# Where the weight clamps of two fused mixers run: VectorE for the first mixer, POOL a step ahead for the second

## The chip, the cores and the metric

One core of a Trainium2 chip runs the whole program. Times are device microseconds (us) of one launch. The kernel before takes 677.71 us (median of 3 runs, 677.46 to 679.39). The core's engines are TensorE (PE, with its weight loads as PEld), VectorE (DVE), ScalarE (ACT), GpSimd (POOL) and SyncE (SP, which here issues every DMA). Each engine takes its own instructions strictly in order; engines wait for one another through semaphores.

## The reference

Shapes: batch 4, 8 heads, 768 tokens, 48 numbers a head; DM = 384, FF1 = 1024, FF2 = 1536.

```
# 1 attention: a decaying state per head
for t in range(S):
    cur = u * k_t (outer) v_t;  y_t = r_t . (state + cur);  state = w * state + k_t (outer) v_t
# 2 first mixer
h = max(x @ w_in, 0);  conv = sum of 3 taps of h along the tokens, weights conv_w
x = (h * sigmoid(conv)) @ w_out
# 3 second mixer
xn = (x - mean) / sqrt(var + 1e-6) * g_ln
out = x + max(xn @ w_ch1, 0) @ w_ch2
```

The inputs of the mixers' weights are 64-bit floating point numbers, which no engine multiplies. They are loaded as pairs of 32-bit words, and the kernel makes 32-bit numbers of them itself.

## The kernel before

The 3072 tokens are 24 tiles of 128 for attention (`attn_tile`, `state_update`) and 8 blocks of 384 for the mixers. All of attention and of the first mixer comes first, interleaved: block j of `mixer1` starts when its three tiles are done, and `step()` pushes the attention of later tiles in between. The results of the first mixer go to DRAM (`x1_dram`). Then the second mixer (`mixer2`) runs over the 8 blocks. It loads each block back (`x1b`, three pieces, `prefetch`), normalises it (`norm`: statistics on DVE, the power -1/2 on POOL as `rs`, the scaled `xn` on DVE), transposes it on PE (`pxt`) and multiplies.

A product of two 32-bit matrices is made of three PE products: each operand is split in a high part that PE takes exactly (`wih`, `woh`, `c1h`, `c2h`, and `xh`, `gh`, `rh`) and a low rest (`wil` and so on).

Weights come in 22 pieces (`wjob`), in this order: three pieces of the first half of w_in (512 columns), one of w_out (`wo_0`), three of the second half of w_in, three of w_out, six of w_ch1 (`c1`), six of w_ch2 (`c2`). All but the w_in pieces are 768 wide. A piece is loaded by SP into a staging tile `st` and then decoded in `wdec` by: ACT, absolute value of the high word read as a 32-bit number; POOL, a clamp to a range (`magnitude`, line 115); DVE, two shifts in one instruction (TENSOR_SCALAR), then two instructions that merge in the low word and the sign (SCALAR_TENSOR_TENSOR); ACT, the rounded high part; DVE, the low rest. The three conv taps go the same way once (`conv_weights`, 24 wide).

Order of this work: `wdo(count, last)` runs so many steps of the current piece, `need(job)` runs steps until a piece is done. In the code before, a piece is three steps, and its ACT and POOL instructions are written right behind the last decode step of the piece ahead of it (`ahead`). After four tiles of attention `wdo` has done the three first w_in pieces and `wo_0`. In block 0 `need` holds features 4 to 7 (`psm` number 4 and on) until the second half of w_in is ready. Instructions that go through `vo`, `ao`, `so`, `go` and all of PE keep the order in which they are written; between them a scheduler places the rest of each engine's instructions beforehand. `ps_m`, `ps_c` and `ps_a` are the PSUM pools.

Of the kernel before, what the change touches and what calls it, by code (L numbers as in the profile page):

```python
# [10 lines left out]
I32 = mybir.dt.int32  # L11
AF = mybir.ActivationFunctionType
ALU = mybir.AluOpType
# [3 lines left out]
DM = H * D  # L17
# [3 lines left out]
NF1 = FF1 // 128  # L21
NF2 = FF2 // 128
# [9 lines left out]
WN = 768  # L32
# [5 lines left out]
W_MIN = 2.0 ** -15 * 1.125  # L38
W_MAX = float.fromhex("0x1.dffcp+16")
# [4 lines left out]
def body(ctx, tc, r, k, v, w, u, w_in, conv_w, w_out, g_ln, w_ch1, w_ch2, out):  # L44
# [4 lines left out]
    io = ctx.enter_context(tc.tile_pool(name="io", bufs=2))  # L49
# [23 lines left out]
    vo = InOrder(nc.vector)  # L73
# [34 lines left out]
    def words(st, n):  # L108
        return [st[:, 0:2 * n].rearrange("p (n two) -> p n two", two=2)[:, :, i] for i in range(2)]

    def magnitude(st, n):

        t = ap.tile([128, WN], F32, tag="wd", name="wdec", bufs=2)[:, 0:n]
        ao.activation(out=t, in_=words(st, n)[1].bitcast(F32), func=AF.Abs)
        go.tensor_scalar(out=t, in0=t, scalar1=W_MIN, scalar2=W_MAX, op0=ALU.max, op1=ALU.min)
        return t

    def decode(st, n, t):
# [9 lines left out]

    wjobs = []

    def wjob(src, n, hi, lo, scale=None):

        st, mag = [], []

        def load():
            st.append(io.tile([128, 2 * WN], I32, tag="st", name="st", bufs=3))
            dst = st[0][:, 0:2 * n]
            if len(src.shape) == 3:
                dst = dst.rearrange("p (a n) -> p a n", a=src.shape[1])
            so.dma_start(out=dst, in_=src.bitcast(I32))  # L140

        def ahead():
            if not mag:
                mag.append(magnitude(st[0], n))

        def steps():
            ahead()
            t = mag[0]
            yield from decode(st[0], n, t)
            if me + 1 < min(len(wjobs), w_loaded[0]):  # L150
                wjobs[me + 1][2]()
            if len(src.shape) == 3:
                t = t.rearrange("p (a n) -> p a n", a=src.shape[1])
            kw = {} if scale is None else {"scale": gl[:, scale:scale + 1]}
            ao.activation(out=hi, in_=t, func=AF.Copy, **kw)
            yield
            if scale is None:
                vo.tensor_tensor(out=lo, in0=t, in1=hi.bitcast(F32), op=ALU.subtract)
            else:
                vo.scalar_tensor_tensor(out=lo, in0=t, scalar=kw["scale"], in1=hi.bitcast(F32),  # L160
                                        op0=ALU.mult, op1=ALU.subtract)
        me = len(wjobs)
        wjobs.append((load, steps(), ahead))
        return len(wjobs) - 1

    wi_job, wo_job, c1_job, c2_job = {}, {}, {}, {}

    def rows2(w_, f):
        return w_[f * 128:f * 128 + 256, :].rearrange("(a p) d -> p a d", p=128)

    def wi_half(f0):
        for kt in range(KT):
            wi_job[f0 // 512] = wjob(w_in[kt * 128:kt * 128 + 128, f0:f0 + 512], 512,
                                     wih[:, kt, f0:f0 + 512], wil[:, kt, f0:f0 + 512])

    def wo_rows(f):
        wo_job[f] = wo_job[f + 1] = wjob(rows2(w_out, f), 2 * DM, woh[:, f:f + 2, :], wol[:, f:f + 2, :])

    wi_half(0)
    wo_rows(0)  # L180
# [13 lines left out]
    def wload(count):  # L194

        while w_loaded[0] < min(count, len(wjobs)):
            wjobs[w_loaded[0]][0]()
            w_loaded[0] += 1

    def wdo(count=1, last=None):  # L200

        for _ in range(count):
            while w_done[0] < (len(wjobs) if last is None else last + 1):
                wload(w_done[0] + 2)
                if next(wjobs[w_done[0]][1], "end") != "end":
                    break
                w_done[0] += 1
# [436 lines left out]
        return cst  # L644

    def conv_weights(cst):
        t = magnitude(cst, 3 * NF1)
        yield from decode(cst, 3 * NF1, t)
        v_.tensor_copy(out=cw, in_=t.rearrange("p (k f) -> p k f", k=3))

# [36 lines left out]
    decayed_k(0)  # L687
    while finished[0] < EARLY - 1:
        step()
        wdo(2, wo_job[0])  # L690
    for _ in conv_weights(cst):
        pass
    ahead, pace = [iter(())], [0]
    for j in range(NB):
        slot = [0]
        while finished[0] < min((j + 1) * TT - (j % 2), NT - 1):
            step()

        def before1(f):
            if f < NF1:  # L700
                need(wi_job[f // 4])
            if f >= LAG - 1:
                need(wo_job[f - LAG + 1])

        def after1(f):
            slot[0] += 1
            pace[0] += 2 if j else 1.9
            if j == 1:
                pace[0] += 0.4
            if pace[0] >= 5:  # L710
                pace[0] -= 5
                step()
            if j == 0:
                wdo(2, wo_job[NF1 - 1])
            elif j < NB - 2:
                wdo(slot[0] % 4 == 0, c1_job[NF2 - 1])
            else:
                wdo(slot[0] % 3 == 0, c2_job[4])
            if j == NB - 1:
                if slot[0] == 1:  # L720
                    ahead[0] = prefetch(0)
                elif slot[0] >= 7:
                    next(ahead[0], None)

        mixer1(xT[j], spill(j), before1, after1)
# [55 lines left out]
```

## Time and profile before

| what | value |
|---|---|
| median of the runs | 677.71 us |
| the profiled execution: its time, its span | 680.46 us, 678.7 us |
| busy: PE, DVE, ACT, POOL | 634.3, 434.7, 268.9, 123.1 us |
| chain that ended last, by engine | PE 62%, DVE 26%, ACT 4%, issue 3%, DMA 2%, POOL 1% |
| POOL clamps of 768, of 512 columns | 16 of 3024 ns and 6 of 2350 ns in the mean |

The span is what the profiler shows between the first and the last instruction; the 1.76 us between it and the execution's time lie around it. A row of the trace's timeline gives the start in us, the duration, the engine, the line of the code, the instruction, what it writes and reads, how many in a row, and in brackets how long the engine stood idle before it and what ended that.

### The profile page before, as it was taken

The page shows a single profiled execution, that of the slowest core. Times are in us where ns is not written, and L with a number is a line of the kernel's source. Part 1 is how long each engine was busy: PE and PEld are TensorE (multiplying, and loading weights), DVE is VectorE, ACT ScalarE, POOL GpSimd, SP SyncE. Part 2 cuts the span into 40 slices and gives each one's busy share as a digit, 9 for nine tenths or more (in the row PEclk, how much of TensorE's full clock was granted, in tenths as well). Part 3 has the DMA queues.
Part 4 walks back from the last instruction along what each step waited for, and adds up shares of the span by engine and source line. Part 5 has one row for each costly group of instructions (what it writes and reads, how often), then busy time and mean ns, then how long its engine had stood idle before and what let it go on. Part 6 is the DMA issues. An engine that isn't in the chain of part 4 may idle for free.

```text
span 678.7 us, 12382 instructions
## 1 busy us (share of the span) xinstructions
PE 634.3 (93%) x5100; PEld 606.8 (89%) x5100; DVE 434.7 (64%) x823; ACT 268.9 (40%) x537; POOL 123.1 (18%) x136
## 2 busy tenths in 40 slices
PE   3758599999989999999999999999999999999996
PEld 3647488899978989999899999999999999999996
DVE  5998999998999899986999624142332415242211
ACT  1436556646565556666675312112121212112110
POOL 5452540412131312301215000000000000000000
PEclk9779699999999999999999999999999999999998
DMA  8964433333334322303033001020201002020001
GB/s 173 181 156 114 150 94 82 67 96 84 84 91 97 82 75 69 94 1 117 1 129 117 0 13 59 1 70 1 71 1 46 25 1 71 1 70 1 36 1 39
DMA packets 93841, 45.14 MB, mean 67 GB/s; under 512 B 80337, under 2 KB 89682, under 8 KB 93778
## 3 DMA queue, kind: packets, MB, share of 16 engines
q1 hardware_dynamic: 93778, 44.28, 25.1%
q8 instruction: 42, 0.69, 0.4%
q14 instruction: 21, 0.17, 0.1%
HBM read 34.83 MB, written 9.44 MB: 65 GB/s over the span
## 4 chain that ended last, share of the span: by engine, by line
PE 62%; DVE 26%; ACT 4%; issue 3%; DMA 2%; POOL 1%; SPq 0%; DVEq 0%; POOLq 0%
PE psm L70 28%; PE acc L70 28%; DVE c L410 6%; DVE wdec L70 4%; DVE aT L285 3%; DVE gl L397 3%; DVE c L391 2%; PE yps L70 2%; DMA x1b<-x_dram 2%; PE dps L70 1%; DVE rT L262 1%; PE pxt L70 1%; POOL wdec L70 1%; DVE av L270 1%; DVE kks L238 1%
## 5 line engine op out<-in xcount | busy, mean ns | idle before, releaser
L424 DVE SCALAR_TENSOR_TENSOR rl<-psm,rh 128x384 fp32r<-128x384 f32 x96 | 53.3, 555 | 142.6 <-ACT rh L423 142.6
L423 ACT ACTIVATE rh<-psm 128x384 fp32r<-128x384 f32 x96 | 47.2, 492 | 207.9 <-PE psm L70 207.9
L70 PE MATMUL psm<-xnh,c1h 128*128 128x384 f32 x288 | 99.0, 344 | 0.1
L70 PE MATMUL psm<-xnh,c1l 128*128 128x384 f32 x288 | 97.5, 338 | 0.0
L70 PE MATMUL acc<-c2h,rh 128*128 128x384 f32 x288 | 97.1, 337 | 0.0
L70 PE MATMUL acc<-c2l,rh 128*128 128x384 f32 x288 | 97.1, 337 | 0.0
L70 PE MATMUL acc<-c2h,rl 128*128 128x384 f32 x288 | 97.0, 337 | 0.0
L70 PE MATMUL psm<-xnl,c1h 128*128 128x384 f32 x288 | 96.9, 337 | 0.0
L410 DVE SCALAR_TENSOR_TENSOR c<-h,cw,c 128x384 f32<-128x384 f32 x128 | 84.5, 661 | 9.1 <-ACT c L408 8.1
L70 POOL TENSOR_SCALAR wdec<-wdec 128x768 f32<-128x768 f32 (+2 forms) x23 | 62.8, 2729 | 115.2 <-ACT wdec L70 93.6
L70 PE MATMUL psm<-xh,wih 128*128 128x386 f32 x192 | 68.9, 359 | 10.7 <-ACT wih L70 7.8
L70 PE MATMUL acc<-woh,gh 128*128 128x384 f32 x192 | 67.4, 351 | 2.3 <-DVE xl L309 1.5
L70 PE MATMUL acc<-woh,gl 128*128 128x384 f32 x192 | 65.6, 341 | 2.7 <-DVE gl L397 2.7
L70 PE MATMUL psm<-xl,wih 128*128 128x386 f32 x192 | 66.2, 345 | 0.0
L70 PE MATMUL psm<-xh,wil 128*128 128x386 f32 x192 | 66.2, 345 | 0.0
L70 PE MATMUL acc<-wol,gh 128*128 128x384 f32 x192 | 65.2, 340 | 0.0
L447 POOL TENSOR_TENSOR rs<-rs,nhalf 128x1 f32<-128x1 f32 x24 | 15.4, 658 | 227.8 <-DVE rs L446 226.4
L390 ACT ACTIVATE c<-c 128x384 f32<-128x384 f32 x64 | 33.5, 524 | 56.2 <-DVE c L410 56.0
L70 PEld LDWEIGHTS psm<-xnh,c1h 128*128 128x128 f32 x288 | 54.3, 189 | 0.4 <-DVE ok L658 0.4
L70 PEld LDWEIGHTS psm<-xnl,c1h 128*128 128x128 f32 x288 | 54.4, 189 | 0.0
L70 PEld LDWEIGHTS psm<-xnh,c1l 128*128 128x128 f32 x288 | 54.2, 188 | 0.0
L70 PEld LDWEIGHTS acc<-c2l,rh 128*128 128x128 f32 x288 | 54.1, 188 | 0.0
(104 smaller groups left out, 1162.1 us busy)
## 6 DMA issues: line engine op xcount, KB each, us to landing
st<-in_moe_w_ch_dram SPq DMA_DIRECT2D x12, 768.0 KB, 4.9
rvbuf<-in_r_dram SPq DMA_DIRECT2D x24, 192.0 KB, 2.9
kt<-in_k_dram SPq DMA_DIRECT2D x24, 192.0 KB, 3.5
rvbuf<-in_v_dram SPq DMA_DIRECT2D x24, 192.0 KB, 3.1
x_dram<-x SPq DMA_DIRECT2D x24, 192.0 KB, 1.9
x1b<-x_dram SPq DMA_DIRECT2D x24, 192.0 KB, 2.9
out_dram<-x1b SPq DMA_DIRECT2D x24, 192.0 KB, 1.9
st<-in_moe_w_in_dram SPq DMA_DIRECT2D x6, 512.0 KB, 5.9
```

Source lines behind the costliest of these rows:

```text
L70: return lambda *args, **kw: tc.keep_in_program_order(op(*args, **kw))
L238: v_.tensor_tensor(out=kks[:, n % 2, :, :, 0:D], in0=loaded[n][1].unsqueeze(1).to_broadcast([128, 2, H, D]), in1=tku, op=ALU.mult)
L262: v_.tensor_tensor(out=rT, in0=prt[0:PR], in1=tr, op=ALU.mult)
L270: v_.tensor_tensor(out=av, in0=kks[:, n % 2, 1, :, 0:D], in1=rt[:, :, 0:D], op=ALU.mult)
L285: v_.copy_predicated(out=aT[:, q], mask=later.bitcast(I32), data=dps[q])
L390: a_.activation(out=st["c"], in_=st["c"], func=AF.Sigmoid)
L391: v_.tensor_tensor(out=st["c"], in0=st["h"][:, 1:T + 1], in1=st["c"], op=ALU.mult)
L397: v_.tensor_tensor(out=st["gl"], in0=st["c"], in1=st["gh"].bitcast(F32), op=ALU.subtract)
L410: v_.scalar_tensor_tensor(out=c, in0=h[:, o:o + T], scalar=cw[:, tap, f:f + 1], in1=c, op0=ALU.mult, op1=ALU.add)
L423: a_.activation(out=gh, in_=ps[:, 0:T], func=AF.Relu)
L424: v_.scalar_tensor_tensor(out=gl_, in0=ps[:, 0:T], scalar=0.0, in1=gh.bitcast(F32), op0=ALU.max, op1=ALU.subtract)
L447: g_.tensor_tensor(out=rs[:, 1:2], in0=rs[:, 0:1], in1=nhalf, op=ALU.pow)
```

## The change

The clamp's engine becomes an argument. The ten pieces of the first mixer and the conv taps give it to DVE; the twelve pieces of the second mixer keep POOL. `ahead` is gone: every piece has a fourth step, which starts it with the absolute value and the clamp, and the piece's decode steps follow in later calls. Pieces of the second mixer are staged in a single tile of their own (`sc`) in place of the three of `st`, and the next one's load is issued in the step of the third decode instruction. The paces of `wdo` change with the step count, and before the first block `wdo` now stops after the three first w_in pieces.

```diff
-    def magnitude(st, n):
+    def magnitude(st, n, clamp):
...
-        go.tensor_scalar(out=t, in0=t, scalar1=W_MIN, scalar2=W_MAX, op0=ALU.max, op1=ALU.min)
+        clamp.tensor_scalar(out=t, in0=t, scalar1=W_MIN, scalar2=W_MAX, op0=ALU.max, op1=ALU.min)
...
-    def wjob(src, n, hi, lo, scale=None):
+    def wjob(src, n, hi, lo, scale=None, clamp=None):
...
-            st.append(io.tile([128, 2 * WN], I32, tag="st", name="st", bufs=3))
+            st.append(io.tile([128, 2 * WN], I32, tag="st" if clamp else "sc", name="st", bufs=3 if clamp else 1))
...
-        def ahead():
-            if not mag:
-                mag.append(magnitude(st[0], n))
-
         def steps():
-            ahead()
-            t = mag[0]
+            t = magnitude(st[0], n, clamp or go)
+            yield
             yield from decode(st[0], n, t)
-            if me + 1 < min(len(wjobs), w_loaded[0]):
-                wjobs[me + 1][2]()
+            if clamp is None:
+                wload(me + 2)
...
     (wi_half and wo_rows: wjob(..., clamp=vo))
...
-                wload(w_done[0] + 2)
+                wload(w_done[0] + (2 if w_done[0] < wo_job[NF1 - 1] else 1))
...
-        t = magnitude(cst, 3 * NF1)
+        t = magnitude(cst, 3 * NF1, vo)
...
-        wdo(2, wo_job[0])
+        wdo(2, wi_job[0])
...
-                wdo(slot[0] % 4 == 0, c1_job[NF2 - 1])
+                wdo(slot[0] % 3 == 0, c1_job[NF2 - 1])
             else:
-                wdo(slot[0] % 3 == 0, c2_job[4])
+                wdo(slot[0] % 2 == 0, c2_job[4])
```

PE's matmuls stand in the same order before and after. What moves on the other engines is shown at three places. The rows give the line, the instruction, what it writes and reads, and its shape; numbers only tell instances of a name apart.

First place: DVE up to the third piece of w_in's second half, which `psm` number 4 needs. Before, the last two of the three pieces are `wdec_645` and `wdec_711`; `c` and `gl` belong to the gates of features 1 to 3.

```order
L70 SCALAR_TENSOR_TENSOR wdec_645<-st_640,wdec_645 128x512
L397 TENSOR_TENSOR gl_824<-c_733,gh_823 128x384
L391 TENSOR_TENSOR c_818<-h_817,c_818 128x384
L70 TENSOR_TENSOR wil_97<-wdec_645,wih_96 128x512
L70 TENSOR_SCALAR wdec_711<-wdec_711 128x512
L397 TENSOR_TENSOR gl_892<-c_818,gh_891 128x384
L70 SCALAR_TENSOR_TENSOR wdec_711<-st_650,wdec_711 128x512 x2
L70 TENSOR_TENSOR wil_97<-wdec_711,wih_96 128x512
```

After, the three pieces are `wdec_695`, `wdec_727` and `wdec_807`, and each begins with two TENSOR_SCALAR, the clamp and the shifts.

```order
L70 SCALAR_TENSOR_TENSOR wdec_695<-st_627,wdec_695 128x512
L387 TENSOR_TENSOR c_795<-h_794,c_795 128x384
L70 SCALAR_TENSOR_TENSOR wdec_695<-st_627,wdec_695 128x512
L258 TENSOR_TENSOR rT_828<-prt_823,tr_85 112x512
L393 TENSOR_TENSOR gl_881<-c_795,gh_880 128x384
L70 TENSOR_TENSOR wil_97<-wdec_695,wih_96 128x512
L70 TENSOR_SCALAR wdec_727<-wdec_727 128x512 x2
L70 SCALAR_TENSOR_TENSOR wdec_727<-st_693,wdec_727 128x512 x2
L70 TENSOR_TENSOR wil_97<-wdec_727,wih_96 128x512
L70 TENSOR_SCALAR wdec_807<-wdec_807 128x512 x2
L70 SCALAR_TENSOR_TENSOR wdec_807<-st_725,wdec_807 128x512 x2
L70 TENSOR_TENSOR wil_97<-wdec_807,wih_96 128x512
```

The clamps have joined DVE's queue, and the last two pieces stand back to back with no gate work between them. The decoding of `wo_0`, which stood ahead of the first `psm`, now stands ahead of these three pieces. Up to the last row DVE's queue holds the same instructions before and after, but for the eight clamps (six of 512, one of 768, one of 24 columns).

Second place: POOL from the end of the first mixer into the second. `rs` is the power of a block's normalisation, `wdec` the clamp of a c2 piece; before:

```order
L70 TENSOR_SCALAR wdec_4135<-wdec_4135 128x768
L70 TENSOR_SCALAR wdec_4335<-wdec_4335 128x768
L70 TENSOR_SCALAR wdec_4468<-wdec_4468 128x768
L447 TENSOR_TENSOR rs_4579<-rs_4579,nhalf_90 128x1
L447 TENSOR_TENSOR rs_4617<-rs_4617,nhalf_90 128x1
L447 TENSOR_TENSOR rs_4655<-rs_4655,nhalf_90 128x1
L70 TENSOR_SCALAR wdec_4518<-wdec_4518 128x768
```

After:

```order
L70 TENSOR_SCALAR wdec_4437<-wdec_4437 128x768
L70 TENSOR_SCALAR wdec_4510<-wdec_4510 128x768
L443 TENSOR_TENSOR rs_4575<-rs_4575,nhalf_90 128x1
L443 TENSOR_TENSOR rs_4616<-rs_4616,nhalf_90 128x1
L443 TENSOR_TENSOR rs_4655<-rs_4655,nhalf_90 128x1
L744 TENSOR_LOAD general_91
L70 TENSOR_SCALAR wdec_4569<-wdec_4569 128x768
```

The two clamps that stand ahead of block 1's three powers are those of the fourth and fifth c2 piece in both. Before, they were staged in tiles of three (`wdec_4335`, `wdec_4468`); after, one by one in the single tile (`wdec_4437`, `wdec_4510`). A read of the flag that chooses a fallback path (TENSOR_LOAD) has come in behind the powers. SP's queue at the same place, where `st` is a c2 piece's load, `x_dram` the store of the last block of the first mixer, and `x1b` the load of block 1; before:

```order
L655 DMA wr<-in_w_dram 1x384
L70 DMA st<-in_moe_w_ch_dram 128x2x768 x2
L681 DMA x1b<-x_dram 128x384 x3
L675 DMA x_dram<-x_4507 128x384
L675 DMA x_dram<-x_4509 128x384
L675 DMA x_dram<-x_4511 128x384
L748 TENSOR_LOAD general
```

After:

```order
L651 DMA wr<-in_w_dram 1x384
L70 DMA st<-in_moe_w_ch_dram 128x2x768
L744 TENSOR_LOAD general
L744 ISA x2
L671 DMA x_dram<-x_4500 128x384
L671 DMA x_dram<-x_4502 128x384
L671 DMA x_dram<-x_4504 128x384
L70 DMA st<-in_moe_w_ch_dram 128x2x768
L677 DMA x1b<-x_dram 128x384 x3
```

The load of the fifth c2 piece (the second `st` after) and the loads of block 1 have moved behind the flag and the three stores. The other engines read the flag in mid-stream now too, PE among its matmuls of block 0.

Third place: DVE at the normalisation of block 0, which runs in the last block of the first mixer. `xn` is the scaled piece that PE's first `pxt` transposes, `c` a tap of a gate. Before (first two of the three `xn`):

```order
L449 TENSOR_SCALAR xn_4221<-x1b_4095,mv_4215,rs_4216 128x384
L410 SCALAR_TENSOR_TENSOR c_4023<-h_4022,cw_88,c_4023 128x384
L449 TENSOR_SCALAR xn_4248<-x1b_4096,mv_4242,rs_4243 128x384
L397 TENSOR_TENSOR gl_3994<-c_3952,gh_3993 128x384
L70 TENSOR_TENSOR c2l0_118<-wdec_3560,c2h0_112 128x768
```

After:

```order
L70 TENSOR_SCALAR wdec_4115<-wdec_4115 128x768
L406 SCALAR_TENSOR_TENSOR c_4163<-h_4162,cw_88,c_4163 128x384
L442 TENSOR_SCALAR rs_4283<-mv_4282 128x1
L406 SCALAR_TENSOR_TENSOR c_4204<-h_4203,cw_88,c_4204 128x384
L445 TENSOR_SCALAR xn_4220<-x1b_4097,mv_4214,rs_4215 128x384
L393 TENSOR_TENSOR gl_4169<-c_4131,gh_4168 128x384
```

The first `xn` has moved behind the first tap of `c_4204`, the gate of the matmul group that PE does last ahead of the first `pxt`; before, that tap (`c_4205`) stands some 30 rows behind it.

## Rows read from the trace of the kernel before

**Rows 1.** Stages: stretch, length, busy PE, PEld, DVE, ACT, POOL, PEclk, DMA, GB/s.

```profile
20.00:49.50 29.50, 18.81 (x305) 15.19 (x302) 26.66 (x45) 10.98 (x22) 17.90 (x17) 0.78 0.81 157
49.50:76.70 27.20, 17.68 (x155) 15.35 (x155) 23.70 (x47) 15.66 (x29) 8.15 (x6) 0.81 0.45 123
...
100.00:320.00 220.00, 214.19 (x2312) 198.56 (x2312) 200.90 (x343) 131.63 (x272) 45.97 (x42) 1.00 0.32 80
...
365.00:678.00 313.00, 307.41 (x1776) 306.01 (x1774) 106.83 (x239) 61.11 (x122) 17.56 (x23) 0.99 0.09 29
```

**Rows 2.** Waits of PE: what waited for what, us in total, times, longest.

```profile
PE psm L70 <- ACT wih L70: 7.8, 2, 5.2
PE psm L70 <- POOL xl L315: 2.8, 1, 2.8
```

**Rows 3.** The same, of 320 to 678 us alone.

```profile
PE acc L70 <- DVE gl L397: 1.0, 1, 1.0
```

**Rows 4.** Timeline: first block's start, last high part of w_in, DVE behind it.

```profile
49.47 0.69 PE L70 MATMUL psm<-xh,wih 128*128 128x386 f32 x1 [2.85 <-POOL xl L315]
...
76.03 0.63 ACT L70 ACTIVATE wih<-wdec 128x512 fp32r<-128x512 f32 x1 [1.72 <-DVE wdec L70]
...
76.69 0.69 DVE L70 TENSOR_TENSOR wil<-wdec,wih 128x512 fp32r<-128x512 f32 x1 [0.69 <-ACT wih L70]
```

**Rows 5.** Timeline of DVE: shifts of 512 columns and the row behind.

```profile
28.50 0.41 DVE L70 TENSOR_SCALAR wdec<-wdec 128x512 int32<-128x512 int32 x1
28.83 0.54 DVE L270 TENSOR_TENSOR av<-kks,rvbuf 128x384 f32<-128x384 f32 x1
```

**Rows 6.** Timeline: DVE rows beside a POOL instruction, and rows of their form alone.

```profile
21.77 1.38 DVE L70 TENSOR_SCALAR wdec<-wdec 128x512 int32<-128x512 int32 x1 [0.83 <-POOL wdec L70]
23.18 0.97 DVE L70 SCALAR_TENSOR_TENSOR wdec<-st,wdec 128x512 int32<-128x512 int32 x1
25.30 0.67 DVE L70 SCALAR_TENSOR_TENSOR wdec<-st,wdec 128x512 int32<-128x512 int32 x1
53.95 1.64 DVE L410 SCALAR_TENSOR_TENSOR c<-h,cw,c 128x384 f32<-128x384 f32 x2 [2.63 <-ACT c L408]
61.38 1.14 DVE L410 SCALAR_TENSOR_TENSOR c<-h,cw,c 128x384 f32<-128x384 f32 x2
74.39 3.00 POOL L70 TENSOR_SCALAR wdec<-wdec 128x768 f32<-128x768 f32 x1 [5.05 <-ACT wdec L70]
74.80 1.19 DVE L70 SCALAR_TENSOR_TENSOR wdec<-st,wdec 128x512 int32<-128x512 int32 x1
```

**Rows 7.** Timeline at block 0's normalisation: the gate's first product, the first transpose.

```profile
343.38 0.64 ACT L408 ACTIVATE c<-h,cw 128x384 f32<-128x384 f32 x1
343.57 0.49 PE L70 MATMUL pxt<-ident,xn 128*128 128x128 f32 x3
```

**Rows 8.** Timeline at block 1's normalisation; then the c2 load's landing.

```profile
366.45 1.38 SPq L675 DMA_DIRECT2D x_dram<-x  x3
368.60 0.46 DVE L449 TENSOR_SCALAR xn<-x1b,mv,rs 128x384 f32<-128x384 f32 x1
370.14 0.72 POOL L447 TENSOR_TENSOR rs<-rs,nhalf 128x1 f32<-128x1 f32 x1 [1.03 <-DVE general L661]
371.13 0.91 ACT L70 ACTIVATE wdec<-st 128x768 f32<-128x768 f32 x1
372.11 0.49 ACT L423 ACTIVATE rh<-psm 128x384 fp32r<-128x384 f32 x1
372.13 2.82 POOL L70 TENSOR_SCALAR wdec<-wdec 128x768 f32<-128x768 f32 x1 [1.28 <-ACT wdec L70]
376.65 0.49 PE L70 MATMUL pxt<-ident,xn 128*128 128x128 f32 x3
```

**Rows 9.** DMA issues of 350 to 385 us: KB each, median us to landing.

```profile
st<-in_moe_w_ch_dram SPq DMA_DIRECT2D x1, 768.0 KB, 4.5
```

**Rows 10.** PE's read of the flag: shortest, median, longest ns; first, last start.

```profile
L748 PEldq TENSOR_LOAD <-general x1: 487/487/487, 669.3 to 669.3; - x1
```

More of the change, by code (lines that the diff above doesn't have):

```diff
@@ L129, in body @@
     wjobs = []
-    def wjob(src, n, hi, lo, scale=None):
-        st, mag = [], []
+    def wjob(src, n, hi, lo, scale=None, clamp=None):
+        st = []
         def load():
-            st.append(io.tile([128, 2 * WN], I32, tag="st", name="st", bufs=3))
+            st.append(io.tile([128, 2 * WN], I32, tag="st" if clamp else "sc", name="st", bufs=3 if clamp else 1))
             dst = st[0][:, 0:2 * n]
@@ L162, in wjob @@
         me = len(wjobs)
-        wjobs.append((load, steps(), ahead))
+        wjobs.append((load, steps()))
         return len(wjobs) - 1
@@ L173, in wi_half @@
             wi_job[f0 // 512] = wjob(w_in[kt * 128:kt * 128 + 128, f0:f0 + 512], 512,
-                                     wih[:, kt, f0:f0 + 512], wil[:, kt, f0:f0 + 512])
+                                     wih[:, kt, f0:f0 + 512], wil[:, kt, f0:f0 + 512], clamp=vo)
     def wo_rows(f):
-        wo_job[f] = wo_job[f + 1] = wjob(rows2(w_out, f), 2 * DM, woh[:, f:f + 2, :], wol[:, f:f + 2, :])
+        wo_job[f] = wo_job[f + 1] = wjob(rows2(w_out, f), 2 * DM, woh[:, f:f + 2, :], wol[:, f:f + 2, :], clamp=vo)
     wi_half(0)
```

## The prediction

> **What bounds the kernel now.** I began with the busy times by stage and looked there for the stages in which PE is not full. From 365 us on PE is busy 307.41 of 313 us, and from 100 to 320 us 214.19 of 220 us, both at the full 2.4 GHz [rows 1]. A weight's clamp can give little back there. From 20 to 76.7 us PE is busy only 36.5 of 56.7 us at a granted clock of about 0.8, while DVE is busy 50.4 of them [rows 1]. So DVE's queue bounds the start, and any gain must come from there. The waits of PE name the two places: 2.8 us for the first `psm`, which starts at 49.47 us, and 7.8 us for the second half of w_in [rows 2]. The last of its three high parts is done at 76.03 + 0.63 = 76.66 us, and PE goes on behind it [rows 4]. I call that moment R. As PE's matmuls keep their order and PE is nearly full behind R, what the start gives or costs is the shift of R.
>
> **The start, up to R.** Up to the third `wil`, DVE's queue holds what it held, and eight clamps more. A clamp is a TENSOR_SCALAR with two constants, as the shifts are. Shifts of 512 columns take 0.41 us, and the row behind starts 0.33 us after them [rows 5], so I take 0.33 for 512 columns, 0.5 for 768 (half as much again) and 0.1 for 24: 6 x 0.33 + 0.5 + 0.1 = +2.6 us. No trace shows this clamp on DVE. If it ran at the pace of the two-input instructions, 0.67 [rows 6], it would cost 0.6 and 0.9 us, which adds 2.0; that is the upper end, and the shifts are the nearer row, being the same instruction on the same tile.
>
> Against it stands what POOL's clamp costs DVE now. DVE waits 0.83 us for the first one; the merge at 23.18 takes 0.97 where the next takes 0.67; the pair of taps at 53.95 takes 1.64 where the pair at 61.38 takes 1.14; the merge at 74.80, inside a 3.00 us clamp, takes 1.19 for 0.68 or so [rows 6]. That is 0.83 + 0.30 + 0.50 + 0.51 = -2.1 us.
>
> The row at 74.80 starts 0.41 us into that clamp and loses half a microsecond of the 2.6 that are left of it [rows 6]. The Trainium skill (SBUF — State Buffer, Who interferes with whom) says that of a VectorE instruction with two SBUF inputs and a GpSimd one that reads SBUF, the second to issue blocks until the first has finished. By that the merge would have stood for 2.6 us and a moved clamp would give that much back; this trace does not agree, so the sum takes 0.51. The same section counts a VectorE tensor_scalar in a two-port mode as a contender, which speaks against this change, and there the trace agrees: the shifts at 21.77 took 1.38 instead of 0.41 beside a POOL selection [rows 6]. By the rule a clamp on DVE can lose 0.97 so as well; I count nothing, since a selection that stops the clamp spares the instruction that it stopped before.
>
> Two more terms. The last two pieces of w_in now stand back to back on DVE, so that DVE waits for ACT's rounding (0.63) behind each; before, one such wait of 0.69 is there [rows 4]: +0.6. And of DVE's 6.3 idle us in the 56.7 [rows 1], 0.83, 2.63 and 0.69 are named above; of the other 2.2 I let 0.6 be filled by the clamps: -0.6. The start is +2.6 - 2.1 + 0.6 - 0.6 = **+0.5 us**. Its ends: the first `psm` will come much earlier, since the decode of `wo_0` has moved behind it (three instructions, by the rows of 512 some 2.4 us for 768 columns) and POOL's queue, which PE waited for there [rows 2], holds no clamp (an estimate of 1.2 us, half a clamp of 512 columns); with three clamps more (-1.0 of it) and the gains at 21.77 and 23.18 (1.1) that is 3.7 us. If nothing of that were lost again before R, the start would be -3.7. But `wo_0` is only moved, and DVE must do it before R all the same. With slow clamps and no idle time filled it is +3.1.
>
> **Behind R.** Three more clamps of w_out (+1.5) meet the loss that POOL's clamps cause there, about 0.5 each by the row at 74.80: nothing. The c1 clamps stay on POOL, a step ahead, and DVE did not wait for them before.
>
> At block 0's normalisation the first `xn` now stands behind the first tap of the gate whose first product ACT gave at 343.38 + 0.64; the first `pxt` ran at 343.57 [rows 7]. ACT has a c2 high part less in front of it after, so I let that product end at 343.25. Tap (0.55) and `xn` (0.46) then end at 344.3: +0.7. Ends: 0, and +1.4 with ACT's time of before.
>
> Loading `x1b` later takes the norm's statistics out of DVE's way around 325 us, where PE waited 1.0 us for `gl` [rows 3]: -1.0, or 0 if another wait takes its place.
>
> At block 1's normalisation the order on POOL is fourth clamp, fifth clamp, powers. The fifth piece's load now stands behind the stores, which SP ended at 366.45 + 1.38 = 367.8. It lands 4.5 us later [rows 9], at 372.4. ACT's `rh` ends at 372.6; then absolute value 0.91, clamp 2.82, power 0.72, `xn` 0.46 [rows 8]: 372.6 + 0.91 + 0.1 + 2.82 + 0.72 + 0.46 = 377.6, where the first `pxt` ran at 376.65, and `xn` had been there since 368.60 + 0.46 [rows 8]. PE waits +1.0. If the single tile is only free when DVE has merged the fourth piece, which I put at 369.2 (its clamp cannot start before ACT is through with the first `rh`), it is 2.2. I take +1.2; the lower end is 0.
>
> PE's read of the flag in mid-stream took 0.487 us where it stands before, at 669.3 [rows 10]. Matmuls already queued can cover it: 0, at most +0.5. The other engines' reads hide in idle time.
>
> Sum: 0.5 + 0.7 - 1.0 + 1.2 = **+1.4 us**. The profiled execution would go from 680.46 to 681.9. It lies 2.75 above the median of the runs, so the predicted median is 677.71 + 1.4 = **679.1 us**. With all low ends it is -3.7 - 1.0 = -4.7, or 673.0; with all high ends 3.1 + 1.4 + 2.2 + 0.5 = +7.2, or 684.9.
>
> **Rivals.** A change of 0.3%, 2.0 us, is about what a measurement of this kernel can tell from none.
>
> *The start wins.* DVE's idle time swallows the clamps and the early `psm` carries through to R: the start keeps 3.0 of its 3.7 us, and the waits at the two norms are small (0 in sum with the wait that goes): 677.71 - 3.0 = 674.7. For it: 2.2 us of idle time without a name, and POOL's 2 to 3 us per clamp leave the chain of each piece. Against it: before, only one clamp of seven made DVE wait, so that latency was mostly hidden, and DVE has 2.6 us more to do.
>
> *The single staged tile makes PE wait.* Its place is block 1's first `pxt`. It decides when the fifth piece lands later than `rh` at 372.6, since each microsecond after that is one of PE's: 2.2 us there, 1.4 at block 0, and the start at +0.5: +4.1, or 681.8. For it: POOL's powers stand behind a clamp whose data is loaded three instructions late. Against it: in 8 us of slack before, only the last part is used up, and the load may land sooner.
>
> *The clamp is slow on DVE.* 0.6 and 0.9 us instead of 0.33 and 0.5: +3.4, or 681.1. Against it stands the shifts' row.
>
> **How the numbers follow.** Forecast, within 2 us of none: 0.42. The start wins: 0.23. Staged tile 0.27 and slow clamp 0.08: together 0.35 slower. So faster 0.23, same 0.42, slower 0.35. The forecast's own range is that of its case, 675.7 to 679.7; the 8 in 10 range reaches to the rivals' times, 674.7 and 681.8, and a little beyond on both sides for the ends above: 674.0 to 682.6.
>
> **What would show it.** In the changed profile: DVE clamps of 0.41 and 0.55 us; the first `psm` at 45 to 47 us, yet the last high part of w_in at 76 to 78; PE with a wait for `xn` or `pxt` of 0.5 to 1.5 us near 344 and 1 to 2 us near 377, seen as DVE waiting for POOL's power and POOL for ACT; no wait of PE for `gl` near 329. I am wrong if R comes before 74 or after 79, if PE waits for neither `pxt`, or if ACT stands waiting for a c1 or c2 load while PE's PSUM fills up, which I have counted at nothing.

## The result: slower, and the profile after

The changed kernel took 684.07 us (median of 4 runs, 683.39 to 684.26) against 677.85 for the kernel before (4 runs, 677.46 to 679.39): a ratio of 1.0086, interval 1.0068 to 1.0103. I had forecast 679.1 and a range up to 682.6. A second set gave 683.93 (8 runs) against 680.15 (31 runs), 1.0045 (1.0028 to 1.0062). The two intervals do not meet, and it is the kernel before whose median differs from set to set (677.85, then 679.8 to 680.6). So the size is 3.8 to 6.2 us by the medians of the two sets; two profiled executions of each kernel, 680.46 and 679.75 before, 684.02 and 684.86 after, put it at 4.3.

The busy times by stage, of the stretches of [rows 1] (length, then PE, PEld, DVE, ACT, POOL, granted clock, DMA share, GB/s):

```profile
20.00:49.50 29.50, 22.97 (x330) 19.35 (x322) 26.36 (x51) 10.36 (x22) 7.88 (x12) 0.83 0.85 164
49.50:76.70 27.20, 15.10 (x138) 12.18 (x137) 26.17 (x48) 15.13 (x28) 1.26 (x1) 0.78 0.43 113
100.00:320.00 220.00, 214.24 (x2307) 197.40 (x2306) 201.82 (x345) 131.07 (x271) 49.08 (x43) 1.00 0.32 80
365.00:678.00 313.00, 308.72 (x1779) 307.12 (x1777) 107.92 (x235) 62.20 (x123) 17.16 (x24) 1.00 0.11 36
```

PE does more ahead of 49.5 us and less behind it; POOL's 26.1 us up to 76.7 have shrunk to 9.1, and DVE's have grown by 2.2. In the last stretch PE is no less busy than before. The waits of PE (us in total, times, longest), answering to [rows 2, 3]:

```profile
PE psm L70 <- ACT wih L70: 5.5, 3, 2.5
PE acc L70 <- ACT woh L70: 4.9, 1, 4.9
PE acc L70 <- DVE wol L70: 1.9, 1, 1.9
PE pxt L70 <- DVE xn L445: 1.7, 2, 0.9
PE psm L70 <- POOL xl L311: 1.5, 1, 1.5
```

The wait for `gl` of [rows 3] is gone and two for `xn` are there, as forecast; that for `woh` is new, 4.9 us. PE's matmuls stand in the same order in both kernels, so a matmul's start can be laid beside that of the same matmul before. By that, with the means of two executions each (us; the single ones in brackets):

| stretch | before | after | change | forecast |
|---|---|---|---|---|
| start to R (last high part of w_in used) | 76.49 (76.71, 76.26) | 77.65 (77.32, 77.98) | +1.2 | +0.5 |
| R to the last `gl` ahead of block 0's norm | 252.5 (252.7, 252.3) | 251.6 (251.9, 251.4) | -0.9 | -1.0 |
| on to block 0's first `pxt` | 14.15 (14.14, 14.16) | 15.05 (14.98, 15.12) | +0.9 | +0.7 |
| on to block 1's first `pxt` | 33.07 (33.08, 33.06) | 34.03 (33.62, 34.43) | +1.0 | +1.2 |
| on to PE's last matmul | 295.55 (both) | 296.36 (296.41, 296.31) | +0.8 | 0 |
| from its start to the end | 6.58 (6.55, 6.61) | 7.96 (8.02, 7.90) | +1.4 | not in the sum |

The four steps that I had worked out sum to +2.2 us where I had +1.4. Two that I had not make another +2.2. The single stretches are less certain than two traces make them look. Two runs further down keep the order of the kernel before on every engine and have other SyncE instructions (e6) or other places of tiles (e12); they take 251.5 and 251.6 us from R to the last `gl` and 34.0 us from block 0's to block 1's `pxt`, where PE has one wait that the first two traces of before do not show (in each):

```profile
PE psm L70 <- DVE ok L658: 1.1, 1, 1.1
```

From R to block 1's `pxt` as a whole the four kernels with the order of before take 299.5 to 299.9 us, and the six with that of the changed kernel 299.7 to 301.0. The start and the two normalisations in the timeline of the changed kernel:

```profile
19.82 1.09 POOL L271 TENSOR_SCALAR_AFFINE_SELECT aT<-a 128x1024 f32<-128x1024 f32 x1 [3.17 <-DVE a L268]
19.89 1.38 DVE L70 TENSOR_SCALAR wdec<-wdec 128x512 f32<-128x512 f32 x1
44.48 0.69 PE L70 MATMUL psm<-xh,wih 128*128 128x386 f32 x1 [1.50 <-POOL xl L311]
50.41 0.55 DVE L70 TENSOR_SCALAR wdec<-wdec 128x768 f32<-128x768 f32 x1
61.34 0.84 ACT L70 ACTIVATE woh<-wdec 128x768 fp32r<-128x768 f32 x1 [2.59 <-DVE wdec L70]
62.24 0.69 PE L70 MATMUL acc<-woh,gh 128*128 128x384 f32 x1 [4.91 <-ACT woh L70]
64.69 0.41 DVE L70 TENSOR_SCALAR wdec<-wdec 128x512 f32<-128x512 f32 x1
73.66 0.69 DVE L70 TENSOR_TENSOR wil<-wdec,wih 128x512 fp32r<-128x512 f32 x1 [0.70 <-ACT wih L70]
77.30 0.69 DVE L70 TENSOR_TENSOR wil<-wdec,wih 128x512 fp32r<-128x512 f32 x1 [0.70 <-ACT wih L70]
77.32 0.69 PE L70 MATMUL psm<-xh,wih 128*128 128x386 f32 x1 [2.23 <-ACT wih L70]
...
343.03 0.60 DVE L406 SCALAR_TENSOR_TENSOR c<-h,cw,c 128x384 f32<-128x384 f32 x1
343.56 0.47 DVE L445 TENSOR_SCALAR xn<-x1b,mv,rs 128x384 f32<-128x384 f32 x1
344.17 0.52 PE L70 MATMUL pxt<-ident,xn 128*128 128x128 f32 x3 [0.91 <-DVE xn L445]
...
367.04 1.36 SPq L671 DMA_DIRECT2D x_dram<-x  x3
367.12 0.95 DVE L70 SCALAR_TENSOR_TENSOR wdec<-st,wdec 128x768 int32<-128x768 int32 x1
368.50 0.40 SPq L70 DMA_DIRECT2D st<-in_moe_w_ch_dram  x1
368.95 1.44 SPq L677 DMA_DIRECT2D x1b<-x_dram  x3
372.83 0.91 ACT L70 ACTIVATE wdec<-st 128x768 f32<-128x768 f32 x1
373.82 2.77 POOL L70 TENSOR_SCALAR wdec<-wdec 128x768 f32<-128x768 f32 x1 [8.67 <-ACT wdec L70]
374.60 0.56 DVE L440 BATCH_NORM_STATS2 bs<-x1b 128x6 f32<-128x384 f32 x1 [0.68 <-DMA x1b<-x_dram]
376.56 1.59 POOL L443 TENSOR_TENSOR rs<-rs,nhalf 128x1 f32<-128x1 f32 x3
377.26 0.48 DVE L445 TENSOR_SCALAR xn<-x1b,mv,rs 128x384 f32<-128x384 f32 x1
377.80 0.55 PE L70 MATMUL pxt<-ident,xn 128*128 128x128 f32 x3 [0.82 <-DVE xn L445]
```

The clamps take 0.41 and 0.55 us, as the shifts do [rows 5]; two of the ten, both beside a POOL selection, take 1.38 (19.89) and 1.31 us (28.31), as a shift did [rows 6]. The first `psm` is 5 us earlier, and all of it is lost again where PE meets the unfinished `wo_0`: by 62.24 us it is level with the kernel before. At block 0 `xn` follows the tap; at block 1 the powers begin the moment the fifth clamp ends.

The last term lies behind the last matmul, where PE has nothing left and VectorE 0.94 us. What shows it are the waits of SyncE's own sequencer, first before, then after:

```profile
SPq L749 <- SPq L749: 2.6, 1, 2.6
```

```profile
SPq L745 <- SPq L745: 4.7, 2, 2.7
```

SyncE ends with a branch past the fallback path and a list of waits for every semaphore. Behind the branch both stand still for 2.6 to 2.7 us. After, there is a second stop of 2.0 us in the middle of that list, behind its fourth wait.

### The profile page after: what moved, and what is told of

The parts are those of the page before. It is cut to its first block, busy times and chain, and to the rows that moved or that the text cites. A ratio compares the mean times of both kernels' runs of the same rounds, so it can differ in the third digit from the quotient of the medians.

```text
span 682.2 us, 12432 instructions
## 1 busy us (share of the span) xinstructions
PE 637.2 (93%) x5100; PEld 608.4 (89%) x5100; DVE 438.5 (64%) x834; ACT 268.8 (39%) x537; POOL 97.3 (14%) x125
## 4 chain that ended last, share of the span: by engine, by line
PE 60%; DVE 29%; ACT 5%; issue 3%; DMA 2%; SPq 0%; POOL 0%; DVEq 0%; ACTq 0%; POOLq 0%
PE psm L70 28%; PE acc L70 27%; DVE c L406 7%; DVE wdec L70 5%; DVE aT L281 3%; DVE gl L393 2%; DVE c L387 2%; DVE rT L258 1%; DMA x1b<-x_dram 1%; DVE kks L234 1%; PE pxt L70 1%; PE yps L70 1%; ACT c L386 1%; DVE av L266 1%; PE dps L70 1%
## 5 line engine op out<-in xcount | busy, mean ns | idle before, releaser
L406 DVE SCALAR_TENSOR_TENSOR c<-h,cw,c 128x384 f32<-128x384 f32 x128 | 87.0, 682 | 9.6 <-ACT c L404 8.6
L271 POOL TENSOR_SCALAR_AFFINE_SELECT aT<-a 128x1024 f32<-128x1024 f32 x24 | 31.5, 1314 | 167.5 <-DVE a L268 100.3
L70 PEld LDWEIGHTS acc<-c2h,rh 128*128 128x128 f32 x288 | 54.1, 188 | 0.0
```

The source lines that it names most:

```text
L70: return lambda *args, **kw: tc.keep_in_program_order(op(*args, **kw))
L271: g_.affine_select(out=aT.rearrange("x q p c -> x (q p) c"), in_=a8.to_broadcast([128, H, C]), compare_op=ALU.is_equal, fill=0.0, base=0, ...
L406: v_.scalar_tensor_tensor(out=c, in0=h[:, o:o + T], scalar=cw[:, tap, f:f + 1], in1=c, op0=ALU.mult, op1=ALU.add)
```

## The experiments

All times are compared with runs of the kernel before in the same set (ratio with its interval). "Last" is the start of PE's last matmul in the run's trace, "tail" what follows it.

| run | ratio | last, us | tail, us |
|---|---|---|---|
| e0_before_again | 1.0002 (0.9987 to 1.0016) | 671.34 | 6.61 |
| after_again | 1.0045 (1.0028 to 1.0062) | 675.25 | 7.90 |
| e4_late_flag | 1.0086 (1.0073 to 1.0099) | 674.22 | 10.03 |
| e1_three_staged | 1.0020 (1.0010 to 1.0030) | 673.26 | 7.18 |
| e2_only_engine | 1.0002 (0.9987 to 1.0016) | 673.51 | 7.26 |
| e9_three_wo0 | 1.0016 (1.0002 to 1.0030) | 672.17 | 7.17 |
| e5_pad_after | 1.0036 (1.0023 to 1.0050) | 674.82 | 6.51 |
| e6_pad_before | 1.0005 (0.9989 to 1.0022) | 670.71 | 7.41 |
| e10_addresses | 1.0054 (1.0037 to 1.0071) | 674.66 | 7.98 |
| e11_addr_pad | 1.0041 (1.0025 to 1.0057) | 674.37 | 7.08 |
| e12_before_shift | 1.0019 (1.0007 to 1.0031) | 672.79 | 7.06 |
| e13_all_dve | 1.0038 (1.0023 to 1.0052) | 672.92 | 7.67 |
| e14_x1b_first | 1.0052 (1.0032 to 1.0072) | 675.11 | 6.35 |
| e15_best_try | 1.0014 (1.0002 to 1.0026) | 672.32 | 6.22 |

**The two kernels again.** No edit.

> The kernel before, unchanged, for a second profile. The first one (680.46 us) lay 2.6 us above the runs' median of 677.85, while the changed kernel's profile (684.02) lies at its median, so the two traces differ by 3.5 us of span and the runs by 6.2. Both theories: runs within 1.5 us of 677.85. Theory A (the first profile had a disturbance in one place): this trace's span is near 676 us and, laid beside the first one matmul by matmul, it is ahead of it from one place on. Theory B (profiles of this kernel are always some 2.6 us long): span near 678.7 again, and the change's cost as the traces show it is 3.5 us.

> The changed kernel once more, so that its trace and runs stand beside those of the kernel before on one chip. Theory A (the loss lies in the waits of PE and behind its last matmul): the trace's last matmul is 2 to 3 us later than the 671.34 us of the second profile of before and the end behind it takes 8.0 us for 6.56; runs 3.5 to 4.5 us over before. Theory B (the first comparison's 6.2 us holds, and a part of it is in neither place): 5.5 us or more over before.

The runs of e0 came at 680.52, not within 1.5 us of 677.85 as both theories had it. Its span was 678.0 us, and no stretch of the table lies over 0.5 us from the first trace: there was no disturbance in one place. The changed kernel's second trace is 3.9 us later at the last matmul, more than the 2 to 3 expected, and 1.3 behind it; its runs lay 3.8 over before, as theory A had it. What the first comparison has beyond that is in neither trace.

**Parts of the change.** e2 is the kernel before with the clamp's engine alone changed. e1 and e4 are the changed kernel with one part undone:

```diff
 # e1: three shared tiles again, loaded two ahead
-tag="st" if clamp else "sc", name="st", bufs=3 if clamp else 1
+tag="st", name="st", bufs=3
...
-            if clamp is None:
-                wload(me + 2)
...
-wload(w_done[0] + (2 if w_done[0] < wo_job[NF1 - 1] else 1))
+wload(w_done[0] + 2)
 # e4
+    late = const.tile([1, 1], I32, name="late")
+    vo.tensor_copy(out=late, in_=general)
-    flag = nc.values_load(general[0:1, 0:1], ...)
+    flag = nc.values_load(late[0:1, 0:1], ...)
 # e9: e1, and
-        wdo(2, wi_job[0])
+        wdo(2, wo_job[0])
```

> The kernel before with one part of the change: the ten clamps of the first mixer's pieces and that of the conv taps move to VectorE, everything else (started a piece ahead, three staged tiles, paces, c1 and c2 on POOL) stays. My sum for the start was +2.6 us for the clamps and -2.1 for POOL's hold on VectorE: by it 678.0 to 679.0 (the last wait for the second half of w_in ends within 1 us of the 76.66 us of before). Rival (the loss of 6 us is the clamps on VectorE): 683 or more. Rival (the engine alone is a gain, and the steps and staging lose it): under 676.5.

R came at 77.04, 0.55 us behind the mean of before, and the runs show no difference. Moving the clamps is neither the loss nor a gain: the sum of +2.6 and -2.1, which makes +0.5, fits this one trace; its two terms are not shown singly. Over the whole trace VectorE is busy 436.5 us for 434.7, though its eleven clamps (the taps' too) take 5.8.

> The changed kernel with the single staged tile undone: pieces of the second mixer are staged in the three tiles that all pieces share, loaded two ahead. (The flag's reading goes to the end by itself.) If the single tile costs what I forecast at the two normalisations (+0.7 and +1.2 us, in the trace +0.8 and +0.55) and at the end (+1.5): runs at 681 to 682. If the rest of the change (four steps, clamps on VectorE) carries the loss: 683.5 to 684.5. If the single tile carries all of it: 677.9.

1.4 us over the kernel before of its set (1.0020), where I had expected 3 to 4 over 677.9. In its trace PE waits for no `xn`; the stretches to block 0's and block 1's `pxt` are 13.97 and 33.15 us (15.05 and 34.03 in the changed kernel), the wait for `gl` is back (0.8). So both waits for `xn` come with the single tile, and by the runs so does the larger part of the loss. But the waits are not what e1 wins back: R to the last `gl` takes 253.2 us for 251.6, so that R to block 1's `pxt` takes 300.3 for 300.5 and 301.0. The gain lies behind that: 295.17 us for 296.36 up to the last matmul, and a tail of 7.18 for 7.96.

> The changed kernel with one thing undone: the flag is read at the end again (from a copy that VectorE makes last), so no engine reads it in mid-stream. In the changed kernel the last matmul is 2.0 us later than before and the end of the program another 1.5 us later: SyncE stands from 678.56 to 680.58 us between two of its last instructions, with an instruction transfer in flight. Theory A (the flag's place sets what SyncE and POOL fetch at the end): the tail behind the last matmul goes from 8.0 to about 6.5 us, runs at 682.5. Theory B (the flag in mid-stream delays the matmuls and the block 1 loads behind it): block 1's first transpose comes 0.5 to 1 us earlier against the matmuls ahead of it, runs at 683. Rival (the flag has no part in it): 684.1 as the changed kernel, tail 8 us.

Wrong on the tail: it grew to 10.03 us, since now every engine reads the flag only when VectorE has made the copy, and SyncE still stops (1.8 us). But the last matmul starts at 674.22 us, within the two traces of the changed kernel (674.20 and 675.25). The flag in mid-stream costs PE nothing that these traces show, as forecast.

> Two parts of the change undone: the pieces of the second mixer in the three shared tiles (as in the run with three staged, 1.0020 of before), and the decoding of the first w_out piece back ahead of the first block. What is left is the clamps on VectorE and the four steps. If moving that piece cost nothing, as I forecast: 1.002 again, the first matmul of the mixer back near 49 us, the last high part of w_in at 77 to 78. If PE's wait of 4.9 us for that piece's high part was a loss of the move: the last high part of w_in 1 us or more earlier, 1.000 or less.

The first `psm` stayed at 44.54, not near 49. This does not clear the place of `wo_0`: with four steps a piece its decoding starts only at 44.36 us in e9 too, so that it is again not ahead of the first `psm`:

```profile
44.36 0.57 DVE L70 TENSOR_SCALAR wdec<-wdec 128x768 f32<-128x768 f32 x1
44.54 0.69 PE L70 MATMUL psm<-xh,wih 128*128 128x386 f32 x1 [2.41 <-POOL xl L309]
47.01 1.93 DVE L70 SCALAR_TENSOR_TENSOR wdec<-st,wdec 128x768 int32<-128x768 int32 x2
```

In e2, where it does stand ahead and POOL has none of these clamps, the first `psm` is at 49.19. The last high part was used at 76.85 for 77.78 in e1, but the runs (1.0016 and 1.0020) do not tell the two apart. The matmul that waits for `woh` in the changed kernel (62.24 us there) shows more: from it to R all eleven traces with four steps a piece take 15.05 to 15.09 us, with `wo_0` early (e9, e15) or late, and the five with three steps (before, e0, e2, e6, e12) 13.9 to 14.5.

**The end of SyncE's stream.** Empty instructions at its start, and nothing else:

```diff
+    for _ in range(8):        # e6: range(10), in the kernel before; e11: range(12), in e10
+        nc.sync.drain()
     with _tile.TileContext(nc, **_TILE) as tc:
```

> The changed kernel with eight empty instructions (DRAIN) at the start of SyncE's stream, and nothing else. SyncE's stream has 559 instructions in the kernel before and 577 in the changed one; its stop at the end falls ahead of the 560th in the changed kernel (2.0 us), ahead of the 560th in the one with the late flag (575, 1.8 us), ahead of its 561st in the two with 564 (1.0 us), and there is none in the kernel before, whose stream ends there. Theory: there a new piece of SyncE's code has to be fetched in the middle of the list of last waits. With 585 the whole list of 22 lies behind that place, and the branch fetches it: the stop goes, the stretch behind the last matmul falls from 8.0 to 6.1 to 6.6 us, runs 1 to 2 us less than the changed kernel's (the empty instructions cost up to 0.5 at the start). Rival (the stop is a wait for the stores or chance): 8.0 us and no gain.

> The kernel before with ten empty instructions (DRAIN) at the start of SyncE's stream, and nothing else: 569 instead of 559, so that the 560th is the 13th of the 22 last ones. Theory: a stop of 1 to 2 us appears ahead of the 13th, the stretch behind the last matmul goes from 6.55 to 7.5 to 8.5 us, runs 1 to 2.5 us over before (up to 0.6 of it at the start). Rival: no stop, runs within 0.6 us of before.

SyncE's own waits at the end, first of e5, then of e6:

```profile
SPq L745 <- SPq L745: 3.0, 1, 3.0
```

```profile
SPq L749 <- SPq L749: 3.6, 2, 2.8
```

In e5 one wait is left, that of the branch; the tail is 6.51 us for 8.02, and the runs 1.0 us less than those of the changed kernel in the same set, part of the gain being spent at the start (the first matmul came 0.4 us later). In e6 a stop appeared ahead of the thirteenth wait of the list, where it was expected, but of 0.5 us only; the second wait in the row is one for the last stores, which landed at 5.3 us. The tail grew by 0.8, below the 1 to 2 expected, and the runs can't tell. Over all kernels the stop falls ahead of the same place in SyncE's stream, and how long it is goes by how early the list gets there (us, from the waits in the traces, less the pace of the list; the counts are those on record, and for e9, 567, three more than e1's 564, as in the traces):

| SyncE's instructions | 559 | 564 | 565 | 567 | 569 | 573 | 575 | 577 | 585, 586 |
|---|---|---|---|---|---|---|---|---|---|
| stop | none | 0.9, 1.0 | 0.8 | 1.1 | 0.5, 1.3 | 1.5 | 1.7 | 1.9 | none (four kernels) |

SyncE goes on 6.1 to 6.6 us behind the last matmul's start, whichever instruction is next (e4 apart, whose list starts 2 us later). In the changed kernel the last transfer of the instruction queue ahead of that ends at 5.2 us, and it goes on at 6.4. That its code comes in pieces, and that this place begins one, fits every row; this is argued, and the fetching itself I have not measured. Without a stop the end can still be late: in e11 SyncE is done 6.24 us behind the last matmul's start, and VectorE only at 7.08.

**Where tiles lie.** In the changed kernel two of each nine w_ch1 matmuls of the second mixer were clearly slower (start to next start, mean of the last 77 groups of nine): the sixth 181.9 ns for 176.3, the eighth 175.2 for 170.6. The fifth lost 2.6 ns, and the ninth won as much.

```diff
-    nhalf = const.tile([128, 1], F32, name="nhalf")
+    nhalf = const.tile([128, 513], F32, name="nhalf")[:, 0:1]   # e12: 769, in the kernel before
```

> The changed kernel with one constant tile (nhalf, 4 bytes a partition) made 2052 bytes wide, of which 4 are used. That changes no instruction, but where tiles lie: the w_ch1 tiles begin at 152,896 bytes of a partition again, as in the kernel before (162,112 in the changed kernel); the flag's reading also goes to the end by itself on PE, VectorE and ScalarE, and SyncE's stream has 573 instructions for 577. Two matmuls of each nine of the second mixer were slower in the changed kernel: the sixth 176 to 182 ns, the eighth 170.6 to 175.2, some 0.8 us over blocks 1 to 7, which took 296.3 to 296.8 us from the first transpose of block 1 to the last matmul for 295.55 before. Theory (addresses): the eighth goes back to 170 to 171, that stretch to 295.2 to 295.6. Rival (something in the changed kernel's order): 175, 296.3. Either way the waits for xn stay at 1.7 to 2.7 us, a stop at the end of SyncE's stream stays, runs at 1.003 to 1.005.

> The kernel before with the same constant tile 3076 bytes wide. The order on every engine is the same; the w_ch1 tiles begin at 156,000 instead of 152,896 bytes, and SyncE's stream has 565 instructions for 559. Theory (addresses): some matmuls of the nine change their mean by 1 to 5 ns and the stretch from block 1's first transpose to the last matmul, 295.55 us in three traces of this program, moves by 0.1 us or more. Rival: 295.55. By the count a stop of 0.5 to 1.2 us at the end; runs within 2 us of before.

> The kernel with the other addresses, with twelve empty instructions (DRAIN) at the start of SyncE's stream: 585 instead of 573. Both terms that I had counted at nothing are undone at once, and the terms of my forecast stay. Theory (start +1.2, gl -1.2, block 0's norm +0.9, block 1's +0.9 us, and the other two are all that is left): the last matmul within 2.5 us of that of before (671.3 to 672.2), 6.5 us behind it, runs at 1.002 to 1.003. Rival (a part is in neither): 1.004 or more.

My theory of the w_ch1 tiles fell: in e10 they lay where they had lain before, and the eighth stayed at 175.2, the stretch at 296.03. But e12, whose order is that of the kernel before on every engine, went from 295.55 to 296.03, its eighth to 174.7 and its ninth from 178.0 to 174.2. Of these 0.49 us 0.27 are one wait, ahead of the `pxt` at 532.64 us, and the other 0.2 the pace. So the place of tiles in SBUF alone can change the pace of single matmuls by 4 ns and this stretch by some tenths of a microsecond; which tile decides, and whether it was this that cost the changed kernel its 0.8, is open. The stretch is not pace alone: in e2, whose sixth and eighth are those of before (176.3 and 170.4), it is 296.27, 0.6 of it again a wait ahead of that `pxt`. e11 was to leave only the forecast's own terms; the last matmul came 2.2 to 3.0 us after that of before, 0.5 of it the empty instructions, and 1.0041 is over what I expected.

**Block 1's normalisation.** e13 puts the clamps of the second mixer on VectorE too; e14 is e13 with the loads of `x1b` ahead of the step's weight work, e15 is e9 with those clamps, both with 14 empty instructions on SyncE.

```diff
-            t = magnitude(st[0], n, clamp or go)
+            t = magnitude(st[0], n, clamp or vo)
 # e14, in after2
-            wdo(2)
             if f == 1 and j + 1 < NB:
                 ahead[0] = prefetch(j + 1)
-            elif f >= 4:
+            wdo(2)
+            if f >= 4:
```

> The changed kernel with all clamps on VectorE, the twelve of the second mixer too; single tile, four steps and the rest stay. In the changed kernel the fifth c2 clamp (2.77 us on POOL) stands ahead of block 1's powers, which begin the moment it ends (377.69), and PE waits 0.9 to 1.6 us for xn there. Theory (POOL's clamp ahead of the powers is the wait): the powers begin when the statistics are done, near 376.9, and that wait falls by 0.6 to 0.8 us; 12 clamps at some 0.55 us cost VectorE 6.6 us where it is not the bound. The wait at block 0 (behind a gate's tap) stays. Rival (the late loads of x1b make the wait): no change of it. Rival (VectorE becomes the bound in blocks 2 to 7 of the first mixer): 2 us or more later at the first transpose of block 0.

> The kernel with all clamps on VectorE (single tile kept), with the loads of a block's x1b issued ahead of that step's weight work in place of behind it, and fourteen empty instructions at the start of SyncE's stream (586 for 569), so that nothing is fetched in the middle of its last waits. Theory (the late loads of x1b make PE's wait at block 1): the three loads are issued near 358 us, not near 369, the wait for xn there (1.2 us) goes, from block 0's first transpose to block 1's it takes 33.1 us for 34.6, and the stretch behind the last matmul falls from 7.7 to 6.5 to 7.1; runs at 1.000 to 1.002. Rival (the fourth and fifth piece's decoding on VectorE stands ahead of the statistics): the wait stays at 0.6 us or more.

> The parts that lost are undone together: three shared tiles, the first w_out piece ahead of the first block, and fourteen empty instructions at the start of SyncE's stream; kept are the four steps and all clamps on VectorE. Theory (what is left of the change is worth nothing): runs within 0.2% of the kernel before, the last matmul at 671 to 672.5 us, 6.5 to 7.1 us behind it. If VectorE's clamps relieve it of POOL's contention: the stretch from the last high part of w_in to block 0's gate falls by 2 us as it did with all clamps on VectorE (249.9 for 252.3), last matmul under 670.5, runs 0.2% or more faster. If VectorE has too much: 1.003 or more.

In e13 no clamp stands ahead of the powers, and PE waits all the same, as the rival with the late loads had it. Its timeline:

```profile
371.69 0.56 DVE L440 BATCH_NORM_STATS2 bs<-x1b 128x6 f32<-128x384 f32 x1 [2.91 <-DMA x1b<-x_dram]
374.84 2.29 POOL L443 TENSOR_TENSOR rs<-rs,nhalf 128x1 f32<-128x1 f32 x3 [30.59 <-DVE rs L442]
376.14 0.48 DVE L445 TENSOR_SCALAR xn<-x1b,mv,rs 128x384 f32<-128x384 f32 x1 [0.32 <-POOL rs L443]
376.67 0.55 PE L70 MATMUL pxt<-ident,xn 128*128 128x128 f32 x3 [1.16 <-DVE xn L445]
```

The statistics wait for the loads of `x1b`. e14 issues those at 342.31 us, and the waits of PE from 343 to 380 us become:

```profile
342.31 0.81 SPq L677 DMA_DIRECT2D x1b<-x_dram  x2
...
PE pxt L70 <- DVE xn L445: 1.3, 1, 1.3
PE acc L70 <- DVE gl L393: 0.7, 1, 0.7
PE acc L70 <- ACT gh L392: 0.5, 1, 0.5
```

The one for `xn` left is block 0's; block 1's is gone, which shows its cause. The time is not gone: PE waits for the last gate instead, from block 0's to block 1's `pxt` it still takes 34.95 us where I had expected 33.1, and the runs (1.0052, for 1.000 to 1.002) are no better than e13's. e15 undoes all that I held for a loss, and comes to 1.0014, 0.8 us; as much goes at its start, where the empty instructions put the first matmul at 9.73 us for 8.95. The 2 us that I had thought possible did not come: no version beat the kernel before.

## Why the prediction was wrong

**What held.** The bound of each stage and the four places were right. VectorE took what POOL lost at the start, R moved by about 1 us, the wait for `gl` went, and PE got two waits for `xn`. The rival in which the start wins fell: the first `psm` came earlier than my own low end, and nothing of that reached R. The slow clamp fell too.

**The step that failed** is the sum itself, in two sentences. One takes the profiled execution from 680.46 to 681.9: it carried everything behind block 1's `pxt` over unchanged. I had counted PE's read of the flag there, at 0 (e4 bears that out), and the other engines' reads as hidden, but not what SyncE does behind its branch. The tail cost +1.4 us, and e5 took that away without touching any work. The row for it was at hand: SyncE's waits in the kernel before show a stop of 2.6 us behind the branch, in which it does nothing. The stretch up to the last matmul (+0.8) I had also taken as fixed. The length of the tail follows from the count of SyncE's instructions (577 for 559, and 564 with three tiles in e1), which the diff does not show. That the places of tiles can change the pace e12 shows; what changed it here is open.

The other sentence takes 2.75 us off, because the profiled execution lay so far above the median of the runs. The changed kernel's profiled execution (684.02) lay at the median of its runs (684.07), and in every later set the kernel before has a median of 679.8 to 680.6: three runs with a median of 677.71 were no base to add +1.4 to. Of the 5.0 us between 679.1 and 684.07 this makes 2.8, and the sum (681.9 for 684.02) the rest.

**What was mis-sized or misnamed.** The start was +1.2 for +0.5. The clamps on VectorE make +0.55 of it (e2), as the sum of +2.6 and -2.1 has it. The rest is the term of the two last pieces that stand back to back: in the changed kernel VectorE waits 0.70 us for ScalarE twice, at 73.66 and 77.30, and the waits add 0.7 to before, for which I had +0.6. What did not come are the 0.6 us of idle time that I let the clamps fill. The early first `psm` was forecast for two reasons; that POOL's queue holds no clamp is not enough by itself (49.19 in e2), and the place of `wo_0` remains. I had `wo_0` at nothing for R, which fits e9 and e15: PE's wait of 4.9 us for its high part only gives back the 5 us that the early `psm` had won. e9 reached R 0.9 us earlier than e1, but by being that much ahead at the `woh` matmul, in one trace each.

At block 1 the size came out (+1.0 for +1.2, and `pxt` at 377.80 and 378.93 for the 377.6 of my chain), and in the changed kernel the clamp did end last. But I held it for the only cause, so the size is in part luck: the statistics, which wait for the loads of `x1b` (374.60), were through only half a microsecond before it. The chain that ended last, before and after, has the loads:

```profile
357.94 4.57 DMA x1b<-x_dram
```

```profile
369.49 5.09 DMA x1b<-x_dram
```

The first of the three is issued at 368.95 for 357.94, 11 us later, because SyncE's order has them behind the fifth piece's load, and that behind the three stores. The single tile is read until 368.07 (the merge at 367.12), and the stores are out at 368.40; with three tiles (e1) the loads go out at 347.82. e13 shows that the late loads alone are enough for the wait. The rival of the single tile had the right place and sign, but its price (a fifth piece that lands later than `rh`) did not occur: it landed at 372.74, and ACT took it at 372.83, straight behind `rh`.

**Open** are which tiles' places set the pace of the matmuls, what made it slower in the changed kernel, and why the kernel before ran 2 to 3 us faster in the first set.

## What to carry to other kernels

Of a transfer that a smaller buffer holds back, price first what stands behind it in the same queue: here three loads behind it made PE wait, and the transfer itself did not. A wait that goes is not time that is won: e1 and e14 lost the wait for `xn`, and from R (e1) or from block 0's `pxt` (e14) to block 1's `pxt` they took about as long as the changed kernel; e14's PE waited for gates instead. When work is only moved, look for the first instruction of PE that needs its result, not only for the end of the stage. And in a change worth less than 1%, take the base from many runs, and look at what follows the last matmul and at the pace of unchanged matmuls: the count of SyncE's instructions moved the end by up to 1.5 us (e5), and the places of tiles the last stretch by 0.2 to 0.5 (e12), where the whole change was forecast at 1.4.

## What the runs showed of the hardware

SyncE stands for 0.5 to 2.0 us in the middle of its last waits when its stream has 564 to 577 instructions, and not with 559, 585 or 586; eight empty ones ahead of the same work take the stop away (e5), ten in the kernel before bring one of 0.5 us (e6). Matmuls of one form in an unchanged order ran at 170.6 or 174.7 ns depending on where tiles lie (e12). Eleven clamps moved from POOL (1.9 to 3.7 us each, 0.3 for the small one of the taps) to VectorE take 5.8 us there, and VectorE's busy time grew by 1.8 us only (436.5 for 434.7); the time of the kernel did not change (e2, 1.0002). A clamp or shift on VectorE that starts beside a selection on POOL takes 1.3 to 1.4 us for 0.41 (19.89, 28.31; 21.77 before).
